# A two-part attention kernel on one core: pooled and causal score tiles turned between output halves, and a new order for 2,538 operations

## The chip, the cores and the metric

The kernel runs on 1 core of one Trainium2 chip. The metric is the device time of one launch in microseconds (us), the median of several runs. The engines of a core run side by side, each through its own list of instructions in order: TensorE (PE) for matrix products, VectorE (DVE), ScalarE (ACT), GpSimd (POOL), and SyncE (SP), which here issues the DMA transfers. An engine that needs another's result waits at that instruction, and everything behind it in its list waits too.

## The reference

Two stages in float32; batch 8, 576 positions, 8 heads of 64.

```python
# stage 1: local band plus pooled attention, per head
q_d, k_d, v_d = (mean of q, k, v over groups of 4 positions)       # 144 positions
out_d = sm_attn(q_d, k_d, v_d)
scores = where(abs(i - j) < 4, scale * q @ k.T, -1e9)
x = repeat(out_d, 4) + softmax(scores) @ v                         # [8, 576, 512]
# stage 2: four experts, each a causal attention of one head of 64, the best two per position
logits = x @ w_gate                                                # top 2 of 4, softmax of these
for e in range(4):
    a = softmax(causal(scale * (x @ wq[e]) @ (x @ wk[e]).T))
    out += gate[..., e] * ((a @ (x @ wv[e])) @ wo[e])
```

The outer lines are shortened here; the arithmetic is the reference's.

## The kernel before, in words

The work is cut by batch b (8), by pair of heads c (4 in stage 1) and by pair of experts p (2 in stage 2). The two heads, or experts, of a pair lie in the two halves of the 128 partitions, so that one matmul takes 64 rows, and two run beside each other on the two halves of the array.

Stage 1 for one pair (b, c): local scores `sc` (L521) are masked (L524), their maxima taken (L527), and become the weights `lp`. Q and K are pooled to `qd`, `kd` (L557, L559 on DVE, L561 to L564 on POOL); pooled scores `scd` (L594) get their maxima (L597), a scale (L599) and the exponential (L604), and become `dp`. Both are transposed on TensorE (L377, into `tp`) and copied out of PSUM (L330 on ACT, L332 on DVE, into `pt` and the like); L659 and L665 to L670 multiply them with V. V's pooled form `vd` comes in batch 0 from matmuls (`pv`, L579), and from then on from a raw tile `lr` that one transfer fills with 256 KB (L500) and another with 64 KB (L502), added up at L573 and L574. There are two such tiles, taken in turn. Stage 2 for (b, p): Q and K by L701, V by L747, causal scores `sq` (L853) for tiles of 64 queries in units of two or three, maxima, exponential and normalisation (L873 to L884), transposes, the product with V (L967), and the product with wo (L990, for the last batch L1012).

Which half of the output rows a score matmul writes is free, since the two heads can change places. The pooled tiles t = 0, 1, 2 write half `h ^ (t // 2)` for head h, causal tiles `e ^ (x % 2)` for expert e, x being the place in the unit, local tiles `h ^ (t // 5)`.

All big PSUM tiles share four buffers. All loads and stores go through SP's list: q (L495), k (L496), V (L505), the raw tiles (L500, L502), stores of out (L997).

The order of everything is a table. The program first notes its 2,538 operations with the tiles they read and write; then `schedule` walks through `SEQ`, in which each number is four times the operation's number plus its choice of engine, and -1 stands for a filler: a matmul of zeros (L483) that nobody reads. Instructions are emitted in that order, and each engine's list is its part of it. Seven more matmuls of zeros (L359) open TensorE's list.

Of the kernel before, what the change touches and what calls it, by code (L numbers as in the profile page):

```python
# [191 lines left out]


class Op:
    __slots__ = ("eng", "cost", "fn", "deps", "succ", "allocs", "bufs", "prio", "seq", "n", "at", "who", "kind", "lag", "unit")


class Plan:
# [42 lines left out]
    def schedule(self):  # L241

        out = []
        for x in SEQ:
            o = self.ops[x // 4] if x >= 0 else self.filler()
            o.who = o.eng[x % 4 if x >= 0 else 0]
            out.append(o)
# [882 lines left out]
```

## Time and profile before

| | us |
|---|---|
| median of 3 runs (469.08 to 472.44) | 469.56 |
| the profiled execution's own time | 468.63 |
| its span | 466.9 |
| TensorE busy | 447.1 (96%) |
| VectorE busy | 378.2 (81%) |
| ScalarE busy | 329.3 (71%) |
| GpSimd busy | 307.3 (66%) |

The span is the time from the first to the last instruction of the one profiled execution; 1.73 us lie around it. A busy share is an average over the whole span, so the table alone doesn't tell where an engine that is short of work in one stretch is the bound in another. Matmuls overlap, and their durations are counted from issue to a modelled end, so that consecutive rows of TensorE can add up to more than the clock shows.

### The profile page before, as it was taken

The numbers are of one execution on the slowest core, as the hardware profiler recorded it, in microseconds if no ns is written. First come the engines' busy times: TensorE is split into PE (matmuls) and PEld (weight loads), VectorE is DVE, ScalarE is ACT, GpSimd is POOL, SyncE is SP. The second block draws the span as 40 slices with busy tenths as digits, with TensorE's granted clock in tenths as the row PEclk, the third lists the DMA queues.
The fourth block names the chain that finished last, engine by engine and source line by source line (L and its number), as shares of the span: only waits on it lengthen the run. The fifth ranks groups of instructions, "written<-read, shape, count | busy, mean of one in ns | idle before, by whom it ended". The sixth has DMA issues, their size and how long they took to land.

```text
span 466.9 us, 20310 instructions
## 1 busy us (share of the span) xinstructions
PE 447.1 (96%) x8360; PEld 404.6 (87%) x8360; DVE 378.2 (81%) x1091; ACT 329.3 (71%) x1051; POOL 307.3 (66%) x466
## 2 busy tenths in 40 slices
PE   6989999999997999999999999999999999999996
PEld 2869897899896988999999998998898899998875
DVE  8788898799986999879887988888998687556761
ACT  2889697779854997574886687754887577565863
POOL 8688966697574699646865887759784846224450
PEclk9789999999998999999999999999999999999999
DMA  9575833623334544233525233532624120110122
GB/s 260 168 220 145 216 112 86 166 85 92 125 108 120 149 122 129 71 130 92 149 93 152 77 95 121 160 117 74 210 83 130 51 64 4 52 65 2 39 80 101
DMA packets 43460, 52.70 MB, mean 113 GB/s; under 512 B 3304, under 2 KB 26344, under 8 KB 43368
## 3 DMA queue, kind: packets, MB, share of 16 engines
q1 hardware_dynamic: 43368, 51.40, 37.5%
q8 instruction: 66, 1.08, 1.0%
q14 instruction: 26, 0.21, 0.2%
HBM read 40.90 MB, written 9.44 MB: 108 GB/s over the span
## 4 chain that ended last, share of the span: by engine, by line
PE 79%; DVE 10%; issue 4%; ACT 3%; POOL 2%; DMA 1%; SPq 0%; ACTq 0%; DVEq 0%; POOLq 0%
PE pj L701 16%; PE sq L853 10%; PE po L990 9%; PE o L967 8%; PE pv L747 8%; PE tq L377 5%; PE tp L377 4%; PE o L659 4%; PE sc L521 4%; PE scd L594 3%; PE o L665 2%; PE po L1012 1%; PE pv L579 1%; POOL pr L884 1%; DMA lr<-in_v_dram 1%
## 5 line engine op out<-in xcount | busy, mean ns | idle before, releaser
L884 POOL TENSOR_SCALAR pr<-pr,pst,gt 128x256 f32<-128x256 f32 (+8 forms) x100 | 67.0, 677 | 56.1 <-DVE pst L881 20.1
L876 ACT ACTIVATE pr<-pr,pst 128x192 f32<-128x192 f32 (+8 forms) x144 | 80.0, 558 | 15.8 <-DVE pst L873 15.1
L701 PE MATMUL pj<-xh,wqk_h 128*128 128x320 f32 (+1 forms) x248 | 75.0, 302 | 0.0
L701 PE MATMUL pj<-xl,wqk_h 128*128 128x320 f32 (+1 forms) x248 | 73.2, 295 | 0.0
L701 PE MATMUL pj<-xh,wqk_l 128*128 128x320 f32 (+1 forms) x248 | 72.9, 294 | 0.0
L873 DVE CUSTOM_DVE_ANT_0 pr<-sq,causal_t 128x384 f32<-128x384 f32 (+8 forms) x144 | 63.7, 484 | 8.0 <-PE sq L853 7.5
L853 PE MATMUL sq<-k,q 64*64 64x256 f32 (+6 forms) x768 | 54.8, 375 | 0.4 <-issue 0.4
L701 PEld LDWEIGHTS pj<-xh,wqk_h 128*128 128x128 f32 x248 | 46.6, 188 | 2.6 <-issue 1.2
L701 PEld LDWEIGHTS pj<-xh,wqk_l 128*128 128x128 f32 x248 | 46.6, 188 | 0.0
L701 PEld LDWEIGHTS pj<-xl,wqk_h 128*128 128x128 f32 x248 | 46.6, 188 | 0.0
L684 POOL TENSOR_TENSOR xl<-x,xh 128x576 fp32r<-128x576 f32 x24 | 34.8, 1449 | 15.2 <-ACT xh L683 15.2
L853 PEld LDWEIGHTS sq<-k,q 64*64 64x64 f32 x768 | 33.2, 134 | 10.7 <-issue 1.6
L604 ACT ACTIVATE dp<-scd,dst 128x144 f32<-128x144 f32 x96 | 35.1, 377 | 10.0 <-DVE dst L599 6.9
L542 POOL TENSOR_TENSOR lp<-lp,lst 128x640 f32<-128x640 f32 x24 | 30.7, 1280 | 11.1 <-DVE lst L541 9.0
L747 PE MATMUL pv<-wvg_h,xh 128*128 128x260 f32 x128 | 37.0, 289 | 0.0
L747 PE MATMUL pv<-wvg_l,xh 128*128 128x260 f32 x128 | 36.2, 283 | 0.0
L377 PE MATMUL tq<-ident,pr 64*128 64x64 f32 x736 | 32.9, 228 | 3.3 <-DVE pt L332 2.6
L747 PE MATMUL pv<-wvg_h,xl 128*128 128x260 f32 x128 | 36.0, 281 | 0.0
L330 ACT COPY ptb<-tq 128x384 f32<-128x384 f32 (+4 forms) x68 | 28.8, 489 | 7.6 <-PE tq L377 7.4
L377 PEld LDWEIGHTS tq<-ident,pr 64*128 64x128 f32 x736 | 27.3, 139 | 7.9 <-DVE pt L332 2.7
L990 PE MATMUL po<-oh,wo_h 128*128 128x256 f32 (+1 forms) x112 | 33.9, 303 | 0.0
L990 PE MATMUL po<-ol,wo_h 128*128 128x256 f32 (+1 forms) x112 | 32.9, 294 | 0.0
(180 smaller groups left out, 1435.9 us busy)
## 6 DMA issues: line engine op xcount, KB each, us to landing
lv<-in_v_dram SPq DMA_DIRECT2D x64, 160.0 KB
lq<-in_qT_dram SPq DMA_DIRECT2D x32, 292.0 KB
lk<-in_kT_dram SPq DMA_DIRECT2D x32, 292.0 KB
out_dram<-ot SPq DMA_DIRECT2D x28, 288.0 KB
lr<-in_v_dram SPq DMA_DIRECT2D x28, 256.0 KB
lr<-in_v_dram SPq DMA_DIRECT2D x28, 64.0 KB
wst<-in_wqk_dram SPq DMA_DIRECT2D x1, 1024.0 KB
vx<-vg SPq DMA_DIRECT2D x8, 128.0 KB
```

Source lines behind the costliest of these rows:

```text
L377: T.transpose(ps()[:, 512 * x + z[x]:512 * x + z[x] + 64], data[r, 0:128], ident[r, r])
L542: op("l_nrm", "GV", (pool_tt(n), dve(n)), lambda e: eng[e].tensor_tensor(p(), p(), st[:, :, 2:3].to_broadcast([128, NT, W]), op=OP.mult), ...
L604: A.activation(p()[:, t, :], scs()[:, at * t:at * t + SD], AF.Exp, bias=st[:, t, 4:5], scale=1.0 / 128.0, accum_out=st[:, t, 0:1])
L684: op("xl", "GV", (1360, dve(576)), lambda e: eng[e].tensor_tensor(xl(), x(), xh()[:, 0:S].bitcast(F32), op=OP.subtract), r=[x, (xh, 0)], w ...
L701: T.matmul(ps()[:, H0 + n0:H0 + n1], ww[:, c, w0 + 128 * p:w0 + 128 * p + 128], xx[b, c]()[:, n0:n1], start=(i == 0), stop=(i == 3 * NP - 1))
L747: T.matmul(ps()[:, at:at + 260], xx[b, c]()[:, 128 * t:128 * t + 128], ww[:, c, :], start=(i == 0), stop=(i == 3 * NP - 1))
L853: T.matmul(pss[x][0]()[halves[e ^ (x % 2)], at_of[x] + at + to:at_of[x] + at + to + n1 - n0], q()[r, 64 * t:64 * t + 64], k()[r, n0:n1], s ...
L873: op("s_max", "V", dve(n) + 4, lambda x=x, t=t, n=n, src=src: V.tensor_tensor_reduce(rows_of[t], src(), causal_t[:, S - 64:S + 256] if t = ...
L876: op("s_exp", "A", 281 + n / 1.2, lambda x=x, t=t, n=n: A.activation(rows_of[t], rows_of[t], AF.Exp, bias=st[:, x, 4:5], scale=-1.0, accum ...
L884: op("s_nrm", "GV", (327 + n / 1.2 + max(0, n - 384) * 1.1, 189 + n / 1.92), lambda g, x=x, t=t, n=n: eng[g].tensor_scalar(rows_of[t], row ...
L967: T.matmul(obs[x]()[r, q0:q1], vg()[kr, j, 64 * (2 * p + e):64 * (2 * p + e) + 64], pt()[kr, e, j, q0:q1], start=j == 0, stop=j == len(job ...
L990: T.matmul(ps()[:, H1 + n0:H1 + n1], ww[:, p, 128 * c:128 * c + 128], xx[b, p]()[:, n0:n1], start=(i == 0), stop=(i == 5))
```

## The change

Three things change in the program; the number of operations and what each computes stay.

First, `SEQ` is another list of the same operations. It has 22 fillers where 9 were: 18 of them (before: 8) stand ahead of the second local score, the other four (before: 1) among the first batch's attention. DVE gets 878 operations (before: 880), ACT 533 (522), POOL 317 (326). Of the 28 pairs of transfers that fill a raw tile, 13 stand directly behind one another in SP's list (before: 7); between the two of a pair stand 36 other transfers in all (before: 109).

Second, the number of a pooled score in `SEQ` now carries a bit: with it, all three tiles of that operation write the other half, and the matmuls that use `dp` take their heads from there.

Third, a causal tile's half follows from its number, `1 - t // 2 % 2`, and no longer from its place in the unit; the third tile of the first unit moves to the other bank, and the copies, the gate and the product with V follow. The gate's six copies are grouped in another way.

```diff
 SEQ = [
-    20, 0, 193, 4, 36, 40, 196, 144, 8, 84, ...
+    1152, 36, 2100, 20, 0, 193, -1, -1, -1, -1, -1, 4, ...
 ]
...
-            o.who = o.eng[x % 4 if x >= 0 else 0]
+            o.which = x % 4 if x >= 0 else 0
+            o.who = o.eng[o.which]
...
-        def mm():
-            for i, t in enumerate((0, 1, 2)):
+        def mm(flip):
+            for t in range(3):
                 for h, r in enumerate(halves):
-                    T.matmul(scs()[halves[h ^ (t // 2)], at * t:at * t + SD],
+                    T.matmul(scs()[halves[h ^ (t // 2) ^ flip], at * t:at * t + SD],
                              qd()[r, min(NQD * t, SD - 64):min(NQD * t, SD - 64) + 64], kd()[r, 0:SD] if t else kd()[r, WT:WT + SD], start=True, stop=True)
-        op("down", "T", 385, mm, r=[qd, kd], w=[scs], alloc=[scs, p])
+        FLIP[b, c] = op("down", "TT", 385, mm, r=[qd, kd], w=[scs], alloc=[scs, p])
...
         def avd():
+            heads = [(h ^ scored.which, r) for h, r in enumerate(halves)]
             for x, kr in enumerate(halves):
-                for h, r in enumerate(halves):
+                for h, r in heads:
                     T.matmul(o()[r, 512 * x + SH:512 * x + SH + SD], vd()[kr, 0, r], of_head(pd()[kr], h, PD0, PD1, 3),
                              start=True, stop=False)
...
-                for at, src, i0, i1, f in ((0, lo, 0, 4, e), (1, hi, 0, 4, 1 - e), (8, hi, 4, 5, e)):
-                    A.copy(gt()[r, at:at + 2 * (i1 - i0) - 1:2, :], we[src, i0:i1, f, :])
+                for at, src in ((0, lo), (1, hi)):
+                    a, g = we[src, 0, 1 - e, :], gt()[r, at, :]
+                    A.copy(bass.AP(tensor=g.tensor, offset=g.offset, ap=[list(g.ap[0]), [8, 2], [4, 2], [1, 2]]),
+                           bass.AP(tensor=a.tensor, offset=a.offset, ap=[list(a.ap[0]), [32, 2], [15 + 2 * e, 2], list(a.ap[1])]))
+                A.copy(gt()[r, 8, :], we[hi, 4, 1 - e, :])
...
+    def turned(t):
+
+        return 1 - t // 2 % 2
+
...
-        pss = [(own[0], 0), (own[1], 0) if u == 4 else (own[0], 1), (own[0], 0)][:len(ts)]
+        pss = [(own[0], 0), (own[1], 0) if u == 4 else (own[0], 1), (own[0], 1)][:len(ts)]
...
-                T.matmul(pss[x][0]()[halves[e ^ (x % 2)], at_of[x] + at + to:at_of[x] + at + to + n1 - n0], q()[r, 64 * t:64 * t + 64], k()[r, n0:n1],
+                T.matmul(pss[x][0]()[halves[e ^ turned(t)], at_of[x] + at + to:at_of[x] + at + to + n1 - n0], q()[r, 64 * t:64 * t + 64], k()[r, n0:n1],
                          start=True, stop=True)
...
             for x, jj, q0, to, vv, at, f in tails:
                 for e, r in enumerate(halves):
                     T.matmul(obs[x]()[r, to:to + 64], vv()[halves[x], at, 64 * (2 * p + e):64 * (2 * p + e) + 64],
-                             pt()[halves[x], e, jj, q0:q0 + 64], start=to < z, stop=(x, at) != (1, 1))
+                             pt()[halves[x], e ^ f, jj, q0:q0 + 64], start=to < z, stop=(x, at) != (1, 1))
```

Constants of an earlier planner (`LAG`, `SWX`, `LOCK`, `RATE` and others) that nothing read any more are deleted too, which shifts the line numbers by 8 to 16.

Where the order moves instructions, first TensorE at the start. `wu` are fillers, `sc` local scores, `scd` pooled scores, `pv` the pooled V of batch 0; x20 stands for twenty matmuls of one operation. Before:

```order
L594 MATMUL scd<-kd,qd 64x144 x6
L483 LDWEIGHTS zero
L483 MATMUL wu<-zero 128x512
...
L521 MATMUL sc<-lk,lq 64x64 x20
L594 MATMUL scd<-kd,qd 64x144 x6
L579 MATMUL pv<-lv,pool 128x128 x7
L521 MATMUL sc<-lk,lq 64x64 x20
```

With the change:

```order
L578 MATMUL scd<-kd,qd 64x144 x6
L467 LDWEIGHTS zero
L467 MATMUL wu<-zero 128x512
...
L505 MATMUL sc<-lk,lq 64x64 x20
L563 MATMUL pv<-lv,pool 128x128 x7
L578 MATMUL scd<-kd,qd 64x144 x6
L505 MATMUL sc<-lk,lq 64x64 x20
```

Seven fillers stand between the first pooled and the second local score, where five did, and the second pooled score and `pv` have changed places. Ahead of these rows stand five fillers, the first local score and six fillers; before, one, the score and two.

Then SP around the raw tiles of batch 3. `lr0_95` and `lr1_96` are the two raw tiles, 128x512 the piece of 256 KB, 32x1x512 that of 64 KB. Before (the 256 KB that belong to this `lr0_95` stand three rows above the first row):

```order
L502 DMA lr1_96<-in_v_dram 32x1x512
L496 DMA lk_2938<-in_kT_dram 128x584
L502 DMA lr1_96<-in_v_dram 32x1x512
L495 DMA lq_2941<-in_qT_dram 128x584
L502 DMA lr0_95<-in_v_dram 32x1x512
L505 DMA lv_2809<-in_v_dram 64x5x128
```

With the change:

```order
L486 DMA lr0_95<-in_v_dram 32x1x512
L484 DMA lr0_95<-in_v_dram 128x512
L480 DMA lk_2467<-in_kT_dram 128x584
L479 DMA lq_2493<-in_qT_dram 128x584
L489 DMA lv_2498<-in_v_dram 64x5x128 x2
L486 DMA lr1_96<-in_v_dram 32x1x512
L484 DMA lr1_96<-in_v_dram 128x512
```

The two pieces of a tile stand together now; before, the small one of `lr0_95` stood behind that of the other tile.

Last, SP at the stores of an early batch's output (`ot`). Before:

```order
L505 DMA lv_4946<-in_v_dram 64x5x128 x2
L502 DMA lr0_95<-in_v_dram 32x1x512
L500 DMA lr0_95<-in_v_dram 128x512
L997 DMA out_0_dram<-ot_5101 128x576
L505 DMA lv_4827<-in_v_dram 64x5x128
```

With the change:

```order
L989 DMA out_0_dram<-ot_5137 128x576
L989 DMA out_0_dram<-ot_5178 128x576
L484 DMA lr1_96<-in_v_dram 128x512
L486 DMA lr0_95<-in_v_dram 32x1x512
L484 DMA lr0_95<-in_v_dram 128x512
L989 DMA out_0_dram<-ot_5230 128x576
L989 DMA out_0_dram<-ot_5297 128x576
L486 DMA lr1_96<-in_v_dram 32x1x512
```

Three pieces of raw tiles stand between two pairs of stores, and a fourth behind the second pair, where a store had loads around it.

## Rows read from the trace of the kernel before

**Rows 1.** The page: span, and busy us (share) xinstructions of each engine.

```profile
span 466.9 us, 20310 instructions
PE 447.1 (96%) x8360; PEld 404.6 (87%) x8360; DVE 378.2 (81%) x1091; ACT 329.3 (71%) x1051; POOL 307.3 (66%) x466
```

**Rows 2.** The page: the chain that ended last, by engine.

```profile
PE 79%; DVE 10%; issue 4%; ACT 3%; POOL 2%; DMA 1%; SPq 0%; ACTq 0%; DVEq 0%; POOLq 0%
```

**Rows 3.** Windows: us, busy of PE, PEld, DVE, ACT, POOL, PEclk, DMA, GB/s.

```profile
3.90:10.70 6.80, 4.52 (x102) 2.36 (x99) 6.73 (x19) 1.33 (x4) 5.51 (x11) 1.00 1.09 304
10.70:17.60 6.90, 5.39 (x62) 4.81 (x66) 4.75 (x13) 6.10 (x27) 4.64 (x9) 0.51 0.55 131
17.60:27.80 10.20, 8.63 (x231) 6.99 (x223) 9.44 (x20) 7.60 (x23) 7.39 (x10) 1.00 0.81 252
27.80:31.20 3.40, 3.40 (x87) 3.04 (x85) 3.15 (x11) 2.57 (x9) 2.88 (x4) 0.50 0.55 145
...
31.20:143.40 112.20, 106.06 (x2090) 98.23 (x2082) 97.69 (x265) 86.45 (x279) 80.88 (x104) 1.00 0.46 127
...
143.80:147.20 3.40, 3.40 (x74) 2.98 (x72) 2.00 (x4) 1.31 (x4) 1.32 (x5) 0.51 0.86 260
147.30:445.00 297.70, 295.65 (x5488) 270.28 (x5483) 243.66 (x731) 212.47 (x680) 194.13 (x293) 1.00 0.33 97
```

**Rows 4.** Timeline of startup, PE and DVE: start, us, instruction, [idle before <-releaser].

```profile
6.36 1.26 PE L483 MATMUL wu<-zero 128*128 128x512 bf16 x5
9.06 0.81 PE L521 MATMUL sc<-lk,lq 64*64 64x64 f32 x40 [1.45 <-DVE scd L597]
12.21 1.23 PE L594 MATMUL scd<-kd,qd 64*64 64x144 f32 x12 [2.34 <-DVE qd L557]
13.37 3.35 PE L579 MATMUL pv<-lv,pool 128*128 128x128 f32 x14
16.65 1.20 PE L521 MATMUL sc<-lk,lq 64*64 64x64 f32 x40
17.78 1.83 PE L579 MATMUL pv<-lv,pool 128*128 128x128 f32 x14
...
17.93 0.82 DVE L524 SCALAR_TENSOR_TENSOR lp<-sc,lmask 128x640 f32<-128x640 f32 x1 [2.41 <-PE sc L521]
```

**Rows 5.** The chain in order of time, 130 to 150 us: start, us, what.

```profile
135.64 5.76 DMA lr<-in_v_dram
...
141.43 0.70 DVE lr L573
...
142.61 0.77 DVE pt L332
```

**Rows 6.** Timeline of SP, 125 to 145 us.

```profile
134.47 0.68 SPq L502 DMA_DIRECT2D lr<-in_v_dram  x1
...
135.64 0.62 SPq L502 DMA_DIRECT2D lr<-in_v_dram  x1
```

**Rows 7.** Waits of PE: us in total, times, longest.

```profile
PE tq L377 <- DVE pt L332: 2.6, 1, 2.6
...
PE tp L377 <- POOL lp L542: 1.1, 1, 1.1
```

**Rows 8.** Timeline of POOL, 84 to 91.5 us.

```profile
85.88 1.29 POOL L573 TENSOR_TENSOR lr<-lr 128x512 f32<-128x512 f32 x1 [7.25 <-DMA lr<-in_v_dram]
```

**Rows 9.** Timeline of PE at two units of causal scores and what follows each.

```profile
67.95 0.77 PE L853 MATMUL sq<-k,q 64*64 64x64 f32 x12
68.46 0.83 PE L521 MATMUL sc<-lk,lq 64*64 64x64 f32 x39
...
263.06 1.19 PE L853 MATMUL sq<-k,q 64*64 64x320 f32 x12
264.08 0.66 PE L594 MATMUL scd<-kd,qd 64*64 64x144 f32 x12
```

**Rows 10.** Waits of SP's queue: us in total, times, longest.

```profile
SPq L997 <- ACT ot L330: 89.4, 10, 26.1
```

More of the change, by code (lines that the diff above doesn't have):

```diff
@@ L194 @@
 class Op:
-    __slots__ = ("eng", "cost", "fn", "deps", "succ", "allocs", "bufs", "prio", "seq", "n", "at", "who", "kind", "lag", "unit")
+    __slots__ = ("eng", "cost", "fn", "deps", "allocs", "bufs", "who", "which", "kind", "unit")
 class Plan:
@@ L206, in op @@
         o = Op()
-        o.lag = LAG.get(kind, 0.0)
-        o.kind, o.eng, o.cost, o.fn, o.unit, o.seq = kind, eng, cost, fn, self.unit, len(self.ops)
-        o.prio = 0.0
-        o.deps, o.succ, o.allocs, o.bufs = set(), [], [], []
+        o.kind, o.eng, o.cost, o.fn, o.unit = kind, eng, cost, fn, self.unit
+        o.deps, o.allocs, o.bufs = set(), [], []
         for b in alloc:
@@ L245, in schedule @@
             o = self.ops[x // 4] if x >= 0 else self.filler()
-            o.who = o.eng[x % 4 if x >= 0 else 0]
+            o.which = x % 4 if x >= 0 else 0
+            o.who = o.eng[o.which]
             out.append(o)
         return out
-TICK = 10240 / 3
-MODE = {"local": "quarter", "down": "quarter", "o1": "quarter", "o1d": "quarter", "av": "quarter", "scores": "quarter", "tp": "column", "trans": "column",
-        "q": "dense", "k": "dense", "v": "dense", "wo": "dense"}
-SWX = {(None, "dense"): 75.0, ("dense", None): 25.0, (None, "quarter"): 95.0, ("dense", "quarter"): 95.0,
-       (None, "column"): 95.0, ("dense", "column"): 90.0, ("column", None): 100.0, ("column", "dense"): 92.0,
-       ("column", "quarter"): 95.0, ("quarter", None): 165.0, ("quarter", "dense"): 205.0, ("quarter", "column"): 150.0}
-LAG = {"scores": 85.0, "down": 60.0, "local": 50.0, "o1d": 20.0, "tp": 85.0, "trans": 85.0}
-SWM = {None: 1.2, "quarter": 1.2, "column": 24.6, "dense": 12.0}
-SWB, MARG = 0, 2.0
-LOCK = {"V": {"vd", "xl", "l_sub", "l_nrm", "d_nrm", "xt", "wlo", "s_nrm", "o_lo", "c_ge", "c_pool"},
-        "G": {"vd", "kd", "qd", "l_sub", "l_nrm", "d_nrm", "xl", "xt", "wlo", "o_lo", "g_rank", "g_mask", "g_nrm"}}
-RATE = {"local": 2.1, "down": 1.2, "tp": 1.4, "trans": 1.4, "o1": 2.1, "o1d": 2.2, "av": 2.0, "scores": 2.1}
 F32R_COL, F32R_MM = 0.4167, 13.2
@@ L270, in dense @@
     return n * (F32R_COL * cols + F32R_MM)
-LATP = {"TA": 197.0, "TV": 196.0, "VA": 128.0, "VV": 127.0, "VG": 203.0, "VT": 202.0, "AV": 141.0, "AG": 159.0, "AT": 216.0,
-        "GA": 75.0, "GT": 127.0}
-LAT = {"T": 200.0, "V": 130.0, "A": 150.0, "G": 150.0, "D": 2000.0}
 def dve(n):
@@ L480, in filler @@
         o, ps = Op(), big("wu")
-        o.kind, o.eng, o.cost, o.prio, o.seq = "warm", "T", 216, 0.0, 0
-        o.deps, o.succ, o.allocs, o.bufs, o.lag = set(), [], [ps], [ps], 0.0
+        o.kind, o.eng, o.cost, o.unit = "warm", "T", 216, None
+        o.deps, o.allocs, o.bufs = set(), [ps], [ps]
         o.fn = lambda: T.matmul(ps()[:, :512], zero[:, :128], zero, start=True, stop=True)
@@ L486, in tile_attn_then_moe @@
     plan.filler = filler
-    LQ, LK, LV, LR, XH, XL, LP, LD = {}, {}, {}, {}, {}, {}, {}, {}
+    LQ, LK, LV, LR, XH, XL, LP, LD, FLIP = {}, {}, {}, {}, {}, {}, {}, {}, {}
     def load(b, c):
@@ L619, in s1_down @@
             op("d_nrm", "GVA", (pool_tt(432), dve(432), 921), norm, r=[ST], w=[p])
-        LD[b, c] = (p, vd)
+        LD[b, c] = (p, vd, FLIP[b, c])
     PD0, PD1, PD2, PD3, PD4 = (0, 4), (4, 1), (3, 3), (1, 0), (2, 2)
@@ L630, in s1_out @@
     def s1_out(b, c):
-        p, (dp, vd), lv = LP[b, c], LD[b, c], LV[b, c]
+        p, (dp, vd, scored), lv = LP[b, c], LD[b, c], LV[b, c]
         ps, pt = big("tp"), buf(wk, [128, 2, 5, TQ], "pt", PTB)
@@ L662, in avd @@
         def avd():
+            heads = [(h ^ scored.which, r) for h, r in enumerate(halves)]
             for x, kr in enumerate(halves):
-                for h, r in enumerate(halves):
+                for h, r in heads:
                     T.matmul(o()[r, 512 * x + SH:512 * x + SH + SD], vd()[kr, 0, r], of_head(pd()[kr], h, PD0, PD1, 3),
                              start=True, stop=False)
-            for h, r in enumerate(halves):
+            for h, r in heads:
                 T.matmul(o()[r, SH:SH + SD].rearrange("p (t q) -> p t q", q=NQD)[:, 0:3:2, :], vd()[lo, 1, r],
@@ L927, in s2_trans @@
                 last = runs[-1] if runs else None
-                if last and last[0] == part and last[6] == t % 2 and last[4] != 2 and jj == last[2] + last[1] and q0 == last[3]:
+                if last and last[0] == part and last[6] == turned(t) and last[4] != 2 and jj == last[2] + last[1] and q0 == last[3]:
                     last[1] += 1
                     last[4] = 1
-                elif last and last[0] == part and last[6] == t % 2 and last[4] != 1 and jj == last[2] and q0 == last[3] + 128 * last[1]:
+                elif last and last[0] == part and last[6] == turned(t) and last[4] != 1 and jj == last[2] and q0 == last[3] + 128 * last[1]:
                     last[1] += 1
@@ L934, in s2_trans @@
                 else:
-                    runs.append([part, 1, jj, q0, 0, x, t % 2])
+                    runs.append([part, 1, jj, q0, 0, x, turned(t)])
             def ev(eng, runs=runs, ps=ps):
@@ L958, in s2_av @@
         jobs = ((0, 64, 256), (1, 192, 256)) if part == 0 else ((0, 0, 320), (1, 0, 320), (2, 64, 320), (3, 192, 320))
-        tails = (((1, 0, 0, 0, vx, 0), (0, 0, 0, 128, vg, 1)) if part == 0 else
-                 ((1, 2, 0, 0, vx, 1), (0, 2, 0, 128, vg, 3), (1, 4, 256, 256, vg, 4)))
+        tails = (((1, 0, 0, 0, vx, 0, 1), (0, 0, 0, 128, vg, 1, 0)) if part == 0 else
+                 ((1, 2, 0, 0, vx, 1, 1), (0, 2, 0, 128, vg, 3, 0), (1, 4, 256, 256, vg, 4, 0)))
         z = 64 if part == 0 else 0
@@ L968, in mm @@
                                  pt()[kr, e, j, q0:q1], start=j == 0, stop=j == len(jobs) - 1 and part == 0 and x == 1)
-            for x, jj, q0, to, vv, at in tails:
+            for x, jj, q0, to, vv, at, f in tails:
                 for e, r in enumerate(halves):
                     T.matmul(obs[x]()[r, to:to + 64], vv()[halves[x], at, 64 * (2 * p + e):64 * (2 * p + e) + 64],
-                             pt()[halves[x], e, jj, q0:q0 + 64], start=to < z, stop=(x, at) != (1, 1))
+                             pt()[halves[x], e ^ f, jj, q0:q0 + 64], start=to < z, stop=(x, at) != (1, 1))
         cost = 15 + 1.667 * (sum(q1 - q0 for _, q0, q1 in jobs) + 64 * (len(tails) + 1) // 2) + 8 * (len(jobs) + 1) - 60
@@ L1084, in tile_attn_then_moe @@
     for o in plan.schedule():
-        if len(o.eng) > 1:
+        if o.eng == "TT":
+            o.fn(o.which)
+        elif len(o.eng) > 1:
             o.fn(o.who)
```

279 rows, old and new, of the table SEQ are left out of this document.

## The prediction

> **What bounds the kernel now.** I read the page's first part, then its chain, then a table of windows, and last the timeline and the waits in the windows that have idle time. On the page TensorE is busy for 447.1 of 466.9 us, and no other engine passes 81% [rows 1]. The chain that ended last agrees: 79% PE, 10% DVE, 1% DMA [rows 2]. So the program ends when TensorE has got through its list, and the new order can win only what TensorE loses now: idle time, and time at its lower clock level. The table of windows says where both lie [rows 3]. From 147.3 to 445 us PE is idle for 2.05 of 297.70 us: nothing is to be had there. From 31.2 to 143.4 it is idle for 6.14 of 112.20. In the 27.3 us of startup (3.9 to 31.2) it is idle for 5.36, yet there DVE is the fuller engine: 6.73 + 4.75 + 9.44 + 3.15 = 24.07 us busy. [...]
>
> All sums are made against the profiled execution, 468.63 us; it lies 0.93 below the median of the runs (469.56), so that I add that at the end. What a measurement of this kernel can tell from no change I take as 1%: below 464.86 is faster, above 474.3 slower.
>
> **Part 1, startup.** The timeline shows how DVE, the full engine, loses time [rows 4]. TensorE waits 1.45 and then 2.34 us for DVE, enters the lower clock behind these pauses, runs the first pooled V (pv, 3.35 us against 1.83 for the same 14 passes later) ahead of the third local score, and that score ends at 17.85. DVE has waited 2.41 us for it by 17.93. In the new order there are 13 more fillers, ten of them before the second local score; behind that one now stand pv, the second pooled score and the third local score, so that pv and the pooled score have changed places and the third score still stands behind both. The fillers fill PE's idle 2.28 us of 3.9 to 10.7 and part of the 1.51 after it [rows 3]. If they keep the clock at 1.00, the 5.39 us of PE work in 10.7 to 17.6 take half, and the score is there 2.7 us earlier: DVE's 2.41 us go. I take **-2.4**. The low bound is all of DVE's idle time, 27.30 - 24.07 = -3.2, since no order of DVE's has become shorter. The high bound: five fillers stand before the first local score where one stood; five take 1.26 us in the timeline [rows 4], so four more can bring this score, and all of DVE's chain behind it, 4/5 x 1.26 = 1.0 us later; if the clock falls all the same, that is +1.0. The lower clock of 27.8 to 31.2 I leave: DVE is busy for 3.15 of those 3.40 us [rows 3], so TensorE at full speed would only wait; its bound is -1.7. The loads of the second pair stand earlier in SP's queue, ahead of a weight: 0, since DVE is full.
>
> **Part 2, the raw V tiles.** The one large stall after startup is at 143.4 us. Read the chain backwards [rows 5]: transposes (tq) wait for DVE's pt, which stands in DVE's queue behind vd and lr, the pooling of a raw V tile, which waits for a DMA that took 5.76 us from issue to landing. The tile comes in two pieces, 256 KB and 64 KB. This was the small piece, issued at 135.64 [rows 6]; in SP's list its big piece stands seven places ahead, and among the six transfers between them is another pair's small piece, issued at 134.47, that waited for its own buffer. TensorE waited 2.6 us [rows 7], and behind the pause came 3.40 us at 0.51 [rows 3], which at full clock are 1.7: the stall costs 4.3. A second one is POOL's: 7.25 us of waiting for lr, until 85.88 [rows 8]; TensorE's one wait for POOL's lp, 1.1 us [rows 7], comes behind it, at 90 us. Together 2.6 + 1.7 + 1.1 = 5.4.
>
> In the new order of SP, 13 of the 28 pairs of pieces stand next to each other, where 7 did, and the other transfers between the two pieces of a pair are 36 in all, where they were 109. The stalling pair is one of the 13. Taking late pieces as proportional to what stands between, 5.4 x (1 - 36/109) = **-3.6**. Bounds: -5.4 (both stalls gone) and 0 (both come back at other places).
>
> [...]
>
> **Part 3, the turned halves.** [...] Counted in PE's list, operations that meet on the same half are now 27, where 20 did: 7 x 0.08 = **+0.5**. So the bit, as the table sets it, does not remove these meetings. [...]
>
> [...]
>
> **Part 4, the rest, at nothing.** Three more fillers stand among the first batch's attention: in PE's idle 1.57 us of 17.6 to 27.8 [rows 3]; without that cover 3/5 x 1.26 = +0.8. Work moved between engines (DVE two operations fewer, ACT eleven more, POOL nine fewer): ACT is busy 71%, POOL 66% [rows 1], so that both have room. The regrouped gate copies are six before and after: 0. The last batch's end has the same operations: 0.
>
> **Sum.** -2.4 - 3.6 + 0.5 = -5.5: own time 463.1, on the median 469.56 - 5.5 = **464.1**. With the first two terms at their low bounds (-0.8 and -1.8 more) it is 461.5; with half of part 2 lost (+1.8) it is 465.9.
>
> **Rivals.** *No gain from landing* (B): pieces of lr are late at other places, because what holds them is not their neighbour but the ring of two tiles: SP waits at lr for vd, whoever stands next to it. For it: the piece ahead of the stalling one waited for DVE and both new neighbours wait for the same ring. Against it: the two pieces of the stalling pair now stand together. Then 469.56 - 2.4 + 0.5 = 467.7; with the startup's gain lost too, and its +1.0 paid, 469.56 + 1.0 + 0.5 = 471.1. *More gain* (E): all of DVE's idle time goes (-0.8), both late tiles (-1.8), and the slow window at 27.8 (-1.7): between 464.1 - 4.3 = 459.8 and 461.5. For it: the fillers also reach there; against it: DVE at 93% in that window. *Slower* (D): pieces of lr now stand directly behind the stores of out. SP has waited 89.4 us in all at stores, 26.1 at the longest [rows 10]; in the new list two stores, then three lr pieces, then two stores, then a piece stand together. A piece held so for longer than its lead gives the stall of part 2, 4.3 us each. With two: 464.1 + 8.6 = 472.7, still within 1%; it decides from the third: 464.1 + 12.9 = 477.0. Against it: the stores of the order now waited just as long, at the price of one stall. *The change doesn't do what it says*, that the bit removes meetings on one half, is counted in part 3 already and gives the same sum.
>
> **Chances.** Forecast 0.50, B 0.30, E 0.12, D 0.08. Of the forecast's 0.50, the part above 464.86 is about 0.12. Faster: 0.38 + 0.12 (E) = 0.50. Same: 0.12 + 0.30 = 0.42. Slower: 0.08. The range runs from 460.0 (most of E) to 470.0 (all of B but its end); the forecast's own is 461.5 to 465.9.
>
> **What would show it.** Part 1: the granted clock between 10.7 and 17.6 at 1.00, and DVE's wait for the third local score under 0.5 us. Part 2: no wait of PE for pt or lp over 1 us between 60 and 150 us, and no window at 0.5 in the middle. Part 3: PE's busy time from 147 us on longer by no more than half a microsecond. B shows as waits for lr of the old size; D as lr landings more than 5 us behind a store's issue. It is wrong if PE's busy time in the steady part moves by more than 2 us, since I moved none of that.

## The result: 456.7 us, faster than the range

| | before | changed |
|---|---|---|
| median, us | 470.97 (4 runs) | 456.72 (4 runs, 456.31 to 460.37) |
| profiled execution's own time, us | 468.63 | 456.31 |
| ratio | | 0.9717 (95%: 0.965 to 0.9784) |

The direction was right, the size was not: the forecast was 464.1, its range ended at 460.0. In the two profiled executions 12.3 us have gone, where I counted 5.5.

The page of the changed kernel, which answers to [rows 1] and [rows 2]:

```profile
span 454.5 us, 20339 instructions
PE 442.4 (97%) x8373; PEld 400.6 (88%) x8373; DVE 373.5 (82%) x1099; ACT 335.2 (74%) x1056; POOL 303.8 (67%) x447
...
PE 81%; DVE 10%; ACT 3%; issue 2%; DMA 2%; POOL 1%; SPq 0%; DVEq 0%; POOLq 0%; ACTq 0%
```

TensorE is still the bound. It is busy for 4.7 us less although it does 13 more fillers, and idle for 12.1 us instead of 19.8. The windows of the changed kernel, for [rows 3] (columns as there):

```profile
3.90:10.70 6.80, 6.80 (x106) 3.29 (x106) 5.96 (x18) 1.18 (x4) 4.79 (x10) 1.00 1.02 284
10.70:17.60 6.90, 6.02 (x110) 5.12 (x102) 6.87 (x17) 5.59 (x22) 4.34 (x7) 1.00 0.74 197
17.60:27.80 10.20, 7.90 (x250) 6.00 (x250) 8.09 (x21) 9.68 (x33) 9.81 (x14) 1.00 0.78 258
27.80:31.20 3.40, 2.81 (x50) 2.47 (x49) 3.40 (x11) 2.73 (x10) 2.51 (x2) 1.00 0.89 248
...
31.20:143.40 112.20, 111.33 (x2235) 103.08 (x2231) 101.07 (x278) 89.60 (x288) 88.03 (x120) 1.00 0.49 139
```

None of these windows is at 0.5 any more. From 31.2 to 143.4 PE is idle for 0.87 us, where it was 6.14. Its waits in the changed kernel between 31 and 440 us (us in total, times, longest; the four longest are shown) hold no DMA, no `pt` and no `lp` over 0.5, against [rows 7]:

```profile
PE sc L505 <- issue: 1.1, 1, 1.1
PE o L655 <- issue: 0.8, 2, 0.4
PE sq L845 <- ACT k L314: 0.5, 1, 0.5
PE pv L741 <- ACT dp L588: 0.5, 1, 0.5
```

To place the 12.3 us, I took from both traces the time at which TensorE had streamed the same number of columns, fillers left out:

| stretch of the kernel before | change in it, us |
|---|---|
| up to 60 us | -1.4 |
| 60 to 140 us | -3.0 |
| the stall at 143 us and the lower clock behind it | -4.1 |
| 150 to 453 us | -1.8 |
| from there to the end | -2.0 |

The first two rows hold to about 0.5 us only, because there the same columns stand in another order in the two lists. At 33 us the changed kernel is some 2 us ahead (1.5 and 2.0 in its two repeats, 1.5 to 3 by other ways of counting); by 60 us part of that is given back.

### The profile page after: what moved, and what is told of

It reads as the page before. It is cut to its first block, busy times and chain, and to the rows that moved or that the text cites. A ratio compares the mean times of both kernels' runs of the same rounds, so it can differ in the third digit from the quotient of the medians.

```text
span 454.5 us, 20339 instructions
## 1 busy us (share of the span) xinstructions
PE 442.4 (97%) x8373; PEld 400.6 (88%) x8373; DVE 373.5 (82%) x1099; ACT 335.2 (74%) x1056; POOL 303.8 (67%) x447
## 4 chain that ended last, share of the span: by engine, by line
PE 81%; DVE 10%; ACT 3%; issue 2%; DMA 2%; POOL 1%; SPq 0%; DVEq 0%; POOLq 0%; ACTq 0%
PE pj L686 20%; PE po L982 10%; PE sq L845 9%; PE pv L732 8%; PE o L959 8%; PE tq L361 5%; PE tp L361 4%; PE o L643 3%; PE sc L505 3%; PE scd L578 2%; PE pv L741 2%; PE po L1004 1%; PE o L650 1%; DMA lk<-in_kT_dram 1%; DMA lv<-in_v_dram 1%
## 5 line engine op out<-in xcount | busy, mean ns | idle before, releaser
L876 POOL TENSOR_SCALAR pr<-pr,pst,gt 128x128 f32<-128x128 f32 (+8 forms) x101 | 71.5, 718 | 51.3 <-DVE pst L873 33.0
L868 ACT ACTIVATE pr<-pr,pst 128x448 f32<-128x448 f32 (+8 forms) x144 | 79.9, 558 | 11.7 <-DVE pst L865 11.1
L865 DVE CUSTOM_DVE_ANT_0 pr<-sq,causal_t 128x448 f32<-128x448 f32 (+8 forms) x144 | 64.1, 484 | 5.1 <-PE sq L845 4.9
L845 PE MATMUL sq<-k,q 64*64 64x256 f32 (+6 forms) x768 | 51.8, 371 | 0.5 <-ACT k L314 0.5
L526 POOL TENSOR_TENSOR lp<-lp,lst 128x640 f32<-128x640 f32 x25 | 32.4, 1294 | 8.5 <-DVE lst L525 6.0
L669 POOL TENSOR_TENSOR xl<-x,xh 128x576 fp32r<-128x576 f32 x23 | 32.8, 1425 | 5.1 <-ACT xh L668 5.1
L971 POOL TENSOR_TENSOR ol<-oc,oh 128x256 fp32r<-128x256 f32 (+1 forms) x27 | 22.4, 830 | 16.2 <-ACT oh L970 16.0
L982 PE MATMUL po<-oh,wo_l 128*128 128x256 f32 (+1 forms) x112 | 32.9, 294 | 0.0
```

The costliest lines, as they stand in the source:

```text
L526: op("l_nrm", "GV", (pool_tt(n), dve(n)), lambda e: eng[e].tensor_tensor(p(), p(), st[:, :, 2:3].to_broadcast([128, NT, W]), op=OP.mult), ...
L669: op("xl", "GV", (1360, dve(576)), lambda e: eng[e].tensor_tensor(xl(), x(), xh()[:, 0:S].bitcast(F32), op=OP.subtract), r=[x, (xh, 0)], w ...
L845: T.matmul(pss[x][0]()[halves[e ^ turned(t)], at_of[x] + at + to:at_of[x] + at + to + n1 - n0], q()[r, 64 * t:64 * t + 64], k()[r, n0:n1], ...
L865: op("s_max", "V", dve(n) + 4, lambda x=x, t=t, n=n, src=src: V.tensor_tensor_reduce(rows_of[t], src(), causal_t[:, S - 64:S + 256] if t = ...
L868: op("s_exp", "A", 281 + n / 1.2, lambda x=x, t=t, n=n: A.activation(rows_of[t], rows_of[t], AF.Exp, bias=st[:, x, 4:5], scale=-1.0, accum ...
L876: op("s_nrm", "GV", (327 + n / 1.2 + max(0, n - 384) * 1.1, 189 + n / 1.92), lambda g, x=x, t=t, n=n: eng[g].tensor_scalar(rows_of[t], row ...
```

## The experiments

Runs of one program scatter with a standard deviation of 1 to 2 us, so a term under 1.5 us is hardly settled by time; for such a term I also read the trace of the run. One thing in the traces varies from run to run of the same list: pauses of TensorE for which the profile names no cause (`issue`). The changed kernel has 0.44 us of them at 39 us and 1.07 at 352; its repeat in 6 has 1.13 and 1.54 between 35 and 42 us and 0.80 at 354. Ratios are to the kernel before on the same chip, and "below before" is worked out from the ratio.

**1. The changed kernel again, and each half of the change by itself.** The order alone is the program of before with the new `SEQ`, the bit cut off; the turning alone is the changed program with the old `SEQ`.

> The changed kernel once more, as the measure for the others of this comparison: about 456.7 us, 12 to 14 below the kernel before.

> The new order, with its fillers, in the program of before: pooled and causal tiles write the halves that they wrote before, the bit is dropped. Theory 'order': the turning is worth nothing that counts, so within 0.5 us of the changed kernel, 456.3 to 457.2. Theory 'turning': the 1.7 us that the changed kernel gains evenly between 150 and 430 us come from the halves, so 458.0 or more. The prediction's own term (+0.5 for turning) would have it 0.5 faster than the changed kernel.

> The old order in the changed program: causal tiles turned by pairs, all bits of the pooled scores 0. Theory 'order': the time of before, within 0.5 us. Theory 'turning': 1 to 2 us below before, from PE's busy time between 150 and 430 us.

Measured: again 456.89, ratio 0.9687 (0.9624 to 0.975); order alone 460.29, 0.9754 (0.9689 to 0.982); turning alone 467.52, 0.9926 (0.9893 to 0.996), that is 3.5 us below before. In this round the turning is a gain in both orders (experiment 6 comes back to that). The order carries the larger part.

**2. The new order up to 152 us, and up to 31 us, the old one behind it.**

```diff
-SEQ = before's
+SEQ = before's first 830 (150) numbers, in the order that the new table gives them, fillers included
+      then the rest of before's
```

> In the program of before (no turning): the operations that the old order issues up to about 152 us stand in the new order, with all new fillers; the rest stands as before. Theory 'stages': startup, the late raw V tiles and the lower clock behind them lie in this part and gain what the traces show at the same amount of TensorE work, 8.5 us, and nothing is given back: before - 8.5, about 461. Theory 'given back': the later part waits for what the first no longer holds up (loads, stores), and more than 2 of the 8.5 us are lost again: 463 or more.

> In the program of before: the operations that the old order issues up to about 31 us stand in the new order with its 13 more fillers; the rest as before. By the trace the new order is 2.6 us ahead at the amount of TensorE work that ends this part. Theory 'kept': before - 2.6. Theory 'given back': what follows is bound by DVE and the loads up to 50 us, where the changed kernel was only 1.4 ahead, so before - 1.5 or less.

Measured: to 152 us 461.87, 0.98 (0.9748 to 0.9853), 9.4 us below before: kept in full. To 31 us 466.96, 0.9966 (0.9926 to 1.0006), 1.6 below, with no gain inside the interval; between the two theories the runs don't decide. So some 7 to 8 us come between 31 and 152 us.

**3. One transfer moved.** In the old order the small piece of the stalling raw tile goes right behind its big one.

```diff
-  ... big(3,0), q, v, small(3,1), k, small(3,3), q, small(3,0) ...
+  ... big(3,0), small(3,0), q, v, small(3,1), k, small(3,3), q ...
```

> The kernel before with one transfer moved: the small piece of batch 3's first raw V tile is issued right behind its big piece, six transfers earlier. Theory 'late piece' (the prediction's part 2): the stall at 143 us goes and with it the lower clock behind it, 2.6 + 1.7: before - 4.3. Theory 'ring': the piece waits for its buffer anyway, within 0.5 us of before.

Measured: 467.79, 0.9951 (0.9913 to 0.9988), 2.3 us below before (0.6 to 4.1; the medians differ by 1.4). In its timeline of PE the same transposes wait 0.83 us where they waited 2.6 [rows 7], and the window that follows is at full clock:

```profile
140.91 0.77 PE L366 MATMUL tq<-ident,pr 64*128 64x64 f32 x18 [0.83 <-DVE pt L321]
```

```profile
143.00:147.00 4.00, 4.00 (x93) 3.49 (x86) 3.97 (x14) 2.54 (x11) 2.91 (x8) 1.00 0.62 210
```

That is 1.8 + 1.7 = 3.5 of the 4.3, and the theory 'ring' falls for this tile: one transfer's place in SP's list set a stall and the clock behind it. The rest of the wait (0.83) stays, since DVE still pools that tile right ahead of `pt`. The profiled execution as a whole is only 0.9 us shorter than that of before (467.76); one of the pauses without a cause, 1.36 us at 362 us before, is 2.48 there.

**4. What a meeting on one half costs.** No causal tile is turned; and one tile alone is. Both programs leave out putting the heads back behind it, at the same number of matmuls.

```diff
-  halves[e ^ (x % 2)]
+  halves[e]                                  # no tile turned
```

```diff
-  (own[0], 0)][:len(ts)]        halves[e ^ (x % 2)]
+  (own[0], 1)][:len(ts)]        halves[e ^ (x > 0)]    # the third tile of the unit of three
```

> The kernel before with no causal tile turned at all: expert e always writes half e, so all tiles of a unit meet on the same half; the heads of the odd tiles come out exchanged. By the prediction's part 3 each such meeting costs 0.08 us, and 64 units get one or two more, so before + 5 or more. Theory 'a switch costs': staying on one half is free and it is the change between short passes that costs; then no slower than before, and up to 2.3 faster from the 16 units of three.

> The kernel before with one tile changed: the third tile of the unit of three causal tiles (64 columns) writes the other bank and the other half, the half that the second tile writes; the heads of that tile are not put back. Theory 'third tile': turning gains by this alone, since in the old order the changed program's unit of three took 348 ns from start to next start where before took 490, so 16 units by 0.14 give before - 2.3. Theory 'parity': the gain comes from the meetings between units and operations; then less than 0.5 us here.

Measured: none turned 500.09, 1.0637 (1.055 to 1.0724), 30 us slower; the third tile alone 468.93, 0.9993 (0.9959 to 1.0028). The 0.08 us for a meeting, by which I expected 5 us, were far too small, and the theory that staying on a half is free falls at once. The unit of [rows 9] whose twelve passes took 1.02 us to the next start takes 1.88 with no tile turned:

```profile
275.41 2.05 PE L853 MATMUL sq<-k,q 64*64 64x320 f32 x12
...
277.29 0.54 PE L594 MATMUL scd<-kd,qd 64*64 64x144 f32 x10
```

1.88 is 1.84 times 1.02. In both programs each half of the output gets 1088 columns here, so the total on a half is not what counts. What differs is the single expert: before, 576 of its 1088 columns go to one half and 512 to the other; with no tile turned all 1088 go to one half, 1.89 times 576. So the two times go with the columns on an expert's fuller half, as if what it sends to the other half ran beside them.

The unit of three tiles says the same. Before, one half gets 192 + 64 = 256 columns of an expert and the other 128; with the third tile moved, both get 192. Before:

```profile
61.64 0.66 PE L853 MATMUL sq<-k,q 64*64 64x192 f32 x12
62.13 0.68 PE L594 MATMUL scd<-kd,qd 64*64 64x144 f32 x12
```

The third tile alone:

```profile
59.96 0.56 PE L853 MATMUL sq<-k,q 64*64 64x192 f32 x12
60.33 0.66 PE L594 MATMUL scd<-kd,qd 64*64 64x144 f32 x12
```

The step to the next start falls from 0.49 to 0.37 us, although the second and the third tile now follow each other on the same half, one meeting more. Divided by the columns on an expert's fuller half (320 and 576 in the two units of [rows 9], 256 and 192 here, 1088 with no tile turned), all five steps give 1.6 to 1.9 ns a column.

The page's line of all causal scores (busy us behind the bar) says the same for each program; first the kernel before, then, each in its own fence, none turned, the third tile alone, the turning alone, the new order alone (of the repeat in 6), the new order with the third tile alone (in 6), the changed kernel:

```profile
L853 PE MATMUL sq<-k,q 64*64 64x256 f32 (+6 forms) x768 | 54.8, 375 | 0.4 <-issue 0.4
```

```profile
L853 PE MATMUL sq<-k,q 64*64 64x256 f32 (+6 forms) x768 | 87.2, 366 | 0.0
```

```profile
L853 PE MATMUL sq<-k,q 64*64 64x320 f32 (+6 forms) x768 | 53.1, 377 | 0.2 <-issue 0.2
```

```profile
L833 PE MATMUL sq<-k,q 64*64 64x320 f32 (+6 forms) x768 | 52.5, 376 | 0.5 <-DVE oc L956 0.3
```

```profile
L843 PE MATMUL sq<-k,q 64*64 64x256 f32 (+6 forms) x768 | 54.0, 372 | 0.5 <-ACT k L320 0.5
```

```profile
L843 PE MATMUL sq<-k,q 64*64 64x320 f32 (+6 forms) x768 | 52.3, 372 | 0.5 <-ACT k L320 0.5
```

```profile
L845 PE MATMUL sq<-k,q 64*64 64x256 f32 (+6 forms) x768 | 51.8, 371 | 0.5 <-ACT k L314 0.5
```

32.4 us more with none turned agree with the 30 of the runs. The third tile alone saves 1.7, all of the turning 2.2 to 2.3, in either order; sixteen units of three at 0.12 make 1.9. The line also moves with the order alone: with the halves of before it is 53.2 in the program with the new order up to 152 us, so that only programs of one order are compared. The third tile changes its bank together with its half, and no run separates the two; the columns on the fuller half account for the gain without the bank.

**5. The bit, the fillers, the tail.**

```diff
-SEQ with 17 bits set            # the bit: all 0
-  5, 6, 7 fillers               # the fillers: 1, 2, 5 as before
-  5 fillers ahead of sc         # fewer: 1
-the old order from 426 us on    # the tail: the new order from there, the old up to it
```

> The changed kernel with the bit of all 32 pooled scores at 0 (17 of them are turned in the table); the causal tiles stay turned by pairs. Theory 'causal rule': all that the turning gives comes from the causal tiles, so within 0.7 us of the changed kernel, about 457. [...]

> The changed kernel with the ten new fillers ahead of the second local score left out (8 there, as before); the other four stay. The prediction's part 1: these fillers keep the clock at 1.00 up to 17.6 us; without them the lower clock comes back there and DVE waits again for the third local score, so about 2.4 us slower than the changed kernel. Rival: the order does it without them, since pv and the pooled score have changed places; within 0.5 us, or 0.8 faster, because the first local score comes earlier.

> The changed kernel with four of the five fillers ahead of the first local score left out. In its trace DVE waits 0.77 us for that score, and DVE is full from there on. Theory 'bound': the whole chain behind it comes 0.8 us earlier, about 456. Rival: the clock falls in the longer pause that follows; then slower by 1 us or more.

> In the program of before: the old order up to where the changed kernel is at 426 us, and from there on the new order (the last part of batch 6's and all of batch 7's output). Theory 'tail': TensorE's last matmul is as late as before, but the end follows it after 3.0 us and not 4.6, so before - 1.6. Rival: the tail's gain came with the earlier order, and this ends as before.

Measured against before on that chip: all bits 0 457.54, 0.9702 (0.9674 to 0.9729); without the ten fillers 457.17, 0.969 (0.9672 to 0.9708); fewer 456.57, 0.9684 (0.9657 to 0.9712); the new tail alone 468.19, 0.992 (0.9896 to 0.9944). The first three can't be told from the changed kernel. The bit is worth nothing that shows. Without the ten fillers the clock does fall, yet the time is the same; its windows:

```profile
3.90:10.70 6.80, 4.68 (x102) 2.34 (x99) 6.73 (x22) 1.26 (x4) 4.66 (x10) 1.00 1.00 278
10.70:17.60 6.90, 6.44 (x89) 6.11 (x90) 5.93 (x14) 5.36 (x21) 4.57 (x8) 0.75 0.91 274
17.60:27.80 10.20, 8.59 (x264) 6.44 (x262) 8.83 (x22) 9.70 (x34) 9.70 (x14) 1.00 0.68 226
27.80:31.20 3.40, 2.09 (x36) 1.93 (x35) 3.40 (x11) 3.23 (x12) 3.00 (x3) 1.00 0.89 265
```

TensorE's `pv` there, and DVE's use of the third local score:

```profile
11.16 3.33 PE L551 MATMUL pv<-lv,pool 128*128 128x128 f32 x14 [2.58 <-DMA lv<-in_v_dram]
```

```profile
15.90 0.77 DVE L496 SCALAR_TENSOR_TENSOR lp<-sc,lmask 128x640 f32<-128x640 f32 x1
```

`pv` takes as long as it did before (3.35 us [rows 4]), but it starts at 11.16 instead of 13.37, since it no longer stands behind the pooled score that waits 2.34 us for DVE. So DVE finds the third local score without a wait at 15.90, where before it waited until 17.93; in the changed kernel this is at 16.17. The fillers give and take: with them DVE comes to the first local score 0.9 us later (6.66 against 5.75); without them it waits 1.33 us in three pauses behind the slower passes. DVE is busy for 24.89 of the 27.3 us here, 24.32 in the changed kernel and 24.07 before.

The tail, in the timelines of PE and ACT. Before:

```profile
462.00 0.28 PE L1012 MATMUL po<-ol,wo_h 128*128 128x256 f32 x1
462.32 1.25 ACT L330 COPY ot<-po 128x256 f32<-128x256 f32 x4 [2.93 <-PE po L1012]
```

The changed kernel:

```profile
451.24 0.28 PE L1004 MATMUL po<-ol,wo_h 128*128 128x256 f32 x1
451.56 0.37 ACT L314 COPY ot<-po 128x256 f32<-128x256 f32 x1 [0.34 <-PE po L1004]
```

The new tail alone:

```profile
463.69 0.28 PE L1001 MATMUL po<-ol,wo_h 128*128 128x256 f32 x1
...
464.00 0.37 ACT L319 COPY ot<-po 128x256 f32<-128x256 f32 x1 [0.32 <-PE po L1001]
```

Before, ACT's copy of TensorE's last tile stood ahead of three copies of finished ones, and all four ran after it. Now one is left. The span ends 4.6 us after the last matmul before (466.9 - 462.28), 3.0 in the changed kernel (454.5 - 451.52) and 3.0 with the new tail alone (467.0 - 463.97): 1.6 us. The runs of the new tail gave 3.8 (2.6 to 4.9); where the other 2 come from stays open. Its profiled execution doesn't show them: there the last matmul ends 1.7 us later than before, one of the pauses without a cause being 2.48 us instead of 1.36, and the span is 467.0 against 466.9.

**6. The turning in the new order, in more rounds.**

> The changed kernel, as the measure for the three beside it: about 457 us.

> The new order without any turning, in more rounds. [...] 16 units of three by 0.07 to 0.10 us and some 0.04 for each meeting of other units: the changed kernel + 2 to 3 us. Rival: the 2.6 us were scatter, within 0.7 us of the changed kernel.

> The new order, with only the third tile of the unit of three on the other bank and half (its heads not put back), the other causal tiles and pooled scores as before. Theory 'balance within a unit': 16 x 0.08 = 1.3 us of the turning's gain, so about halfway between the two others. Theory 'alternation between units': the gain is elsewhere, and this is within 0.7 us of the one without turning.

> The changed kernel without four of the five fillers ahead of the first local score, in more rounds. Theory 'bound by DVE': 0.8 us faster than the changed kernel. Theory 'absorbed': startup ends in waits for loads and POOL that this does not move; within 0.5 us.

Measured: again 457.27, 0.9729 (0.9697 to 0.9761); without turning 457.90, 0.9757 (0.9724 to 0.979); the third tile alone 456.97, 0.9738 (0.9705 to 0.9772); fewer fillers 458.20, 0.9749 (0.9706 to 0.9791). By time this round settles nothing: all four lie within their scatter. Over all rounds, 14 runs of the changed kernel and 10 without turning, the means are 457.1 and 459.0, 1.8 us apart with an uncertainty of 1.5 (two standard errors, over several chips), which agrees with the 2.2 us of TensorE's busy time in 4. No version beats the changed kernel by more than the scatter.

## Why the prediction was wrong, point by point

**The base.** I set the sum on a median of 469.56 from three runs. Four runs give 470.97, and the later rounds medians from 469.2 to 472.0. That is no part of the miss but hides some of it: against 470.97 the change is 14.3 us, in the two profiled executions 12.3, where I had 5.5.

**Part 1, startup: the size about held, by luck; the reason did not.** -2.4 was forecast, the changed kernel is some 2 us ahead at 33 us, and the new order up to 31 us alone gave 1.6 +- 1.9. Both signs came, the clock at 1.00 and no wait for the third local score. But I put the gain down to the fillers and the clock, and without ten of the fillers the time is the same at a clock of 0.75. What fails is the step "if they keep the clock at 1.00, the 5.39 us take half": the third score comes early enough without that, because, by the trace of that run, `pv` and the pooled score have changed places, an exchange that I named and gave no price. No run moves these two alone. That five fillers delay the first local score was right, 0.77 us of DVE's waiting in the changed kernel; taking four away gained nothing that shows.

**Part 2, the raw V tiles: right mechanism, too small.** The price of the stall was right: 4.1 went where I had 4.3. The failing step is "late pieces as proportional to what stands between": I took 67% of 5.4, but a stall comes from one tile, and both tiles that were late are on time: before, DVE and POOL waited 13.4 us for raw tiles, in four waits, and in the changed kernel no engine waits for one. So nearly the whole 5.4 goes, my low bound (4.1 + 1.1). That POOL's late tile comes in time by its place alone was not tried by itself. Between 60 and 140 us 3.0 went altogether, POOL's 1.1 among it; TensorE is idle for 2.34 us there before, and of the pauses other than POOL's I had moved none.

**Part 3, the turned halves: wrong in sign.** +0.5 was forecast, 2.2 to 2.3 us of TensorE's time went. I counted meetings at 0.08 us each, an estimate of mine that no run shows; it came from two rows [rows 9] that I had read the wrong way round: the longer unit holds no meeting, since its order is one half, the other, the first; the shorter one, which I took to alternate, begins with 64 and 256 columns on the same half. What makes a unit long is the fuller half: how many columns of one expert fall on it, at 1.6 to 1.9 ns each in experiment 4. The number of meetings, which rose, says little: the unit of three got one more and became shorter, 0.37 us instead of 0.49. Nor does a run show the 0.07 to 0.10 us for a unit of three and the 0.04 for a meeting of other units by which I expected 2 to 3 us in experiment 6: the unit of three gained 0.12 us in experiment 4, and over all rounds the means are 1.8 us apart. The bit, which I thought the heart of it, does nothing that shows; the new place of a third tile with 64 columns does most.

**Part 4: the tail was not 0.** "The last batch's end has the same operations" is true, and beside the point: their order on ACT set 1.6 us behind the last matmul. I compared counts there and not the two lists.

Of the 6.8 us between my 5.5 and the 12.3, part 2 makes 1.6, part 3 2.7 and part 4 1.6, together 5.9; the rest, some 0.9, is of the size of the pauses without a cause and was not traced further.

**The rivals.** E, more gain, was the nearest: both late tiles on time was its main term, though even its 459.8 was too high. D did not come: SP's waits at the stores even grew to 103.3 us, and no raw tile was late for it. B's ring is refuted by experiment 3 for the tile that stalled. My closing test, that it would be wrong if TensorE's busy time in the steady part moved by more than 2 us, is what happened: for the columns streamed between 150 and 453 us before, it is busy for 297.9 us instead of 300.6.

## What to carry to other kernels

Price a stall by what ends it: find the one transfer, ask whether that one moves, and what the engine waits for next when it does (0.83 us in experiment 3). Where small matmuls share the array, take each half of the rows by itself and add up the columns that its neighbouring passes send to either half of the output; in experiment 4 the time went with the fuller one, at 1.6 to 1.9 ns a column in the five steps. Do not count meetings: the unit that got one more took 0.37 us instead of 0.49. And compare the lists of every engine behind the last matmul, since what follows it is part of the span: 4.6 us before, 3.0 with the change.

## What had not been expected

Turning no causal tile raised the busy time of 768 passes from 54.8 to 87.2 us: which half of the output they write is worth more than half as much again as the passes themselves. And without the ten fillers the granted clock was 0.75 from 10.7 to 17.6 us without a loss that shows (457.17 us): the waits of DVE behind the slower passes, 1.33 us, cost about what the fillers against them had cost, 0.9.
